# A fused attention, Fourier mixing and feed-forward kernel: slots replaced by a list scheduler, weights converted in two VectorE passes

## The chip, the cores and the metric

One core of a Trainium2 chip runs the program, in one launch. The metric is device time in microseconds: the median of the runs shown. The core's engines are TensorE (PE in the profile; its weight loads are PEld), VectorE (DVE), ScalarE (ACT), GpSimd (POOL) and SyncE (SP), which issues all DMAs. Each engine works through its own instructions in order and waits on semaphores for the others.

## The reference

```python
# batch 8, heads 8, 512 local and 32 global tokens, head size 64
s_g  = scale * q_g @ concat(k_g, k_l).T          # 32 global queries see everything
out_g = softmax(s_g) @ concat(v_g, v_l)
s_l  = concat(scale * q_l @ k_g.T, where(|i - j| <= 32, scale * q_l @ k_l.T, -1e9))
out_l = softmax(s_l) @ concat(v_g, v_l)
x = concat(out_g, out_l)                         # (8, 544, 512) after joining the heads
u = x + real(fft(fft(x, axis=1), axis=2))        # mixing over tokens and channels
un = (u - mean) / sqrt(var + 1e-6)
out = u + relu(un @ w_ch1) @ w_ch2               # 512 -> 2048 -> 512
```

All is float32 for the host; the weights reach the kernel as pairs of 32-bit words of a 64-bit float, and the kernel converts them itself. For precision nearly every factor of a matmul is a sum of two float16 parts (hi and lo), so that a product takes three matmuls (hi·hi, hi·lo, lo·hi).

## The kernel before

**The stages.** *Attention* goes by pairs of heads, 4 pairs a batch, 32 in all; a pair has 4 units of 128 queries. For a unit: `scores` (PE) into one PSUM tile S, `masked` (line 409, DVE: add the mask, take the row minimum of the negated values), `exps` (line 418, ACT), `p_hi` (422, ACT) and `p_lo` (426, POOL) split the probabilities, `turn` (431, SP) transposes them by DMA into `pl`, `values` (447, 449, PE) multiplies with V into a PSUM bank, `norm` (458 to 460, DVE) divides. S has one buffer for two units and is shared with the global queries' scores (`g_scores`, `g_exp` on lines 482 and 483). Results go to DRAM (`xs`). *The Fourier mixing* of a batch loads `xs` again (lines 582 to 588 and 550 to 559), folds it with additions on DVE and POOL (`d_odd`, `d_even`, `d_tail`), multiplies with cosine and sine tables (`d_first`, `d_second`) and adds into `u`. *The feed-forward* goes by 17 chunks of 256 tokens. A chunk needs statistics, normalised rows (`l_un`, `l_lo` on line 780) turned by DMA (`l_turn`), then 8 steps of `f_first` (line 812: 24 matmuls of 256 columns), `f_hi` (817, ACT), `f_lo` (821, DVE) and `f_second` (831: 12 matmuls of 512 columns), and ends with line 836 and the store.

**The weights** are 32 tiles of 128x512 numbers (16 for each matrix). For a tile, `w_load` (178) fetches 512 KB, `w_abs` (186, ACT) takes the high word's magnitude into PSUM, and `w_bits` makes four passes on DVE (lines 194 to 197): a maximum with an accumulator, a shift, and two that put the bits of a float32 together. `w_max`, `w_fold` and `w_scale` find a power of two for a block of 512 columns by way of a PE transpose. `w_hi` (252, ACT) then makes the hi part. The lo part of the first matrix takes two POOL passes (259, 263), that of the second one DVE pass (261). All 32 tiles of both matrices have to be through before a chunk can end.

**The order.** A table written by hand gives every call a slot and a rank in it; `Plan.run` sorts all calls by that time and records them in this order, and each engine's program is what falls to it. The first chunk has slot 37 (`F0`); each step of the feed-forward has a fixed place between attention steps:

```python
for fp in range(8):
    t = F + 2 * fp
    at(t + .30, self.f_first, c, fp)
    at(t + .97, self.f_hi, c, fp)
    at(t + 1.20, self.f_lo, c, fp)
    at(t + 3.30, self.f_second, c, fp)
```

Counted in PE's order, 1022 matmuls of attention, mixing and scales stand ahead of the first `f_first`, and 3899 behind it; the feed-forward has 3264 on line 812 and 1632 on line 831.

Of the kernel before, what the change touches and what calls it, by code (L numbers as in the profile page):

```python
# [74 lines left out]

class Plan:
    def __init__(self, warp):
        self.q, self.warp = [], warp

    def add(self, slot, rank, fn, *a):  # L80
        self.at(self.warp(slot + rank), fn, *a)

    def at(self, time, fn, *a):
        self.q.append((time, len(self.q), fn, a))

    def run(self):
        for *_, fn, a in sorted(self.q, key=lambda e: e[:2]):
            fn(*a)
# [951 lines left out]
```

## Time and profile before

| | us |
|---|---|
| three runs | 1143.2, 1146.0, 1149.0 (median 1146.0) |
| span of the profiled execution | 1140.9 |
| median less the span | 5.1 |
| first matmul of the feed-forward starts | 219.6 |
| last result of the feed-forward is written | 1132.3 |
| one chunk of 17 where nothing else runs on PE | 41.7 |

The profiled execution's own time, with what lies around its span, is not shown apart; the runs are 2.3 to 8.1 us longer than its span, and the median 5.1. The profile has a page (busy time of each engine, a row of 40 slices), the timeline of instructions, a list of waits with what ended them, groups of equal instructions with their mean, and sums over chosen stretches. In a row of a group, `out<-in` names tiles, and behind the bar stand total busy time, the mean of one in ns, and the idle time before. PE's busy time has modelled ends, so that a stretch that reads 100% busy still can be slower than its matmuls allow; the distance from start to start of a stage is the safer number.

### The profile page before, as it was taken

What the parts mean: (1) busy time and instruction counts of PE and PEld (TensorE: products, weight loads), DVE (VectorE), ACT (ScalarE), POOL (GpSimd) and SP (SyncE); (2) the same over time, 40 slices, a digit from 0 to 9 for tenths busy, and PEclk for the clock granted to TensorE, in tenths of its full rate; (3) what the DMA queues carried; (4) which work ended last, traced back from release to release, by engine and by line L of the source; (5) the groups of instructions that cost most, each with busy time, mean ns of one, the idle gap of its engine ahead of it and who ended that gap; (6) DMA issues with size and microseconds to landing.
All of it is one profiled execution on the core that took longest, in us unless ns stands there. A gap on an engine that the chain in (4) does not pass through costs nothing.

```text
span 1140.9 us, 25333 instructions
## 1 busy us (share of the span) xinstructions
PE 962.4 (84%) x9831; PEld 683.1 (60%) x9831; DVE 715.2 (63%) x1884; ACT 622.1 (55%) x1350; POOL 558.9 (49%) x712
## 2 busy tenths in 40 slices
PE   0244326597999899999999999999999999999996
PEld 0133215465666676667766676766667766666664
DVE  6997898768775847495749574947494453413211
ACT  5768558688676566666656665666564212212210
POOL 3789375758566745574557455645473212201100
PEclk9997556599999999999999999999999999999998
DMA  7478966568569483748365936583645212011100
GB/s 272 148 153 229 272 164 140 137 132 165 119 138 197 68 192 68 180 77 192 65 178 81 178 79 177 81 189 67 132 84 126 52 58 74 16 47 38 19 20 19
DMA packets 249569, 137.63 MB, mean 121 GB/s; under 512 B 200576, under 2 KB 223200, under 8 KB 249448
## 3 DMA queue, kind: packets, MB, share of 16 engines
q1 hardware_dynamic: 249448, 136.01, 52.2%
q8 instruction: 77, 1.26, 0.5%
q14 instruction: 44, 0.36, 0.1%
HBM read 65.10 MB, written 18.35 MB: 73 GB/s over the span
## 4 chain that ended last, share of the span: by engine, by line
PE 51%; DVE 26%; ACT 7%; DMA 7%; issue 4%; POOL 3%; SPq 1%; DVEq 0%; POOLq 0%; ACTq 0%
PE acc L831 21%; PE ps L812 21%; DVE pe L409 2%; ACT pe L418 2%; PE S L399 2%; DMA xt<-xs 2%; DVE h L821 2%; PE bk L708 2%; DVE ps L195 1%; DVE z L329 1%; DVE ps L194 1%; DVE ps L196 1%; PE S L469 1%; DVE z L319 1%; DVE wm L197 1%
## 5 line engine op out<-in xcount | busy, mean ns | idle before, releaser
L812 PE MATMUL ps<-uh,wh 128*128 128x256 f16 x3264 | 382.5, 274 | 0.0
L831 PE MATMUL acc<-wh,h 128*128 128x512 f16 x1632 | 377.8, 381 | 2.3 <-DVE u L836 2.2
L812 PEld LDWEIGHTS <-wh 128*128 128x128 f16 x3264 | 318.8, 98 | 58.9 <-issue 0.6
L831 PEld LDWEIGHTS <-h 128*128 128x128 f16 x1632 | 153.7, 99 | 172.5 <-issue 8.8
L426 POOL TENSOR_TENSOR ph<-pe,ph 128x448 f16<-128x448 f32 x128 | 135.7, 1060 | 162.1 <-ACT ph L422 98.5
L821 DVE SCALAR_TENSOR_TENSOR h<-ps,h 128x512 f16<-128x512 f32 x136 | 93.3, 686 | 184.4 <-ACT h L817 183.9
L817 ACT ACTIVATE h<-ps 128x512 f16<-128x512 f32 x136 | 80.1, 589 | 222.4 <-PE ps L812 222.3
L418 ACT ACTIVATE pe<-pe,nm 128x224 f32<-128x224 f32 x256 | 102.0, 469 | 75.3 <-DVE nm L409 75.2
L409 DVE CUSTOM_DVE_ANT_0 pe<-S,msk,z 128x224 f32<-128x224 f32 x256 | 99.6, 446 | 3.1 <-PE S L399 2.5
L447 PE MATMUL bk<-vN,pl 128*128 128x65 f16 x768 | 72.9, 203 | 31.5 <-DMA pl<-ph 14.6
L399 PE MATMUL S<-kT,qT 64*128 64x192 f16 x768 | 56.5, 273 | 40.1 <-ACT pg L483 35.7
L399 PEld LDWEIGHTS <-qT 64*128 64x128 f16 x1536 | 54.8, 102 | 45.5 <-issue 37.1
L447 PEld LDWEIGHTS <-pl 128*128 128x128 f16 x768 | 62.2, 104 | 22.2 <-DMA pl<-ph 16.6
L422 ACT ACTIVATE ph<-pe 128x448 f16<-128x448 f32 x128 | 72.0, 563 | 0.0
L449 PEld LDWEIGHTS <-pl 96*128 96x128 f16 x768 | 60.0, 104 | 18.5 <-issue 11.7
L765 POOL TENSOR_SCALAR ve<-ve 128x2 f32<-128x2 f32 x17 | 5.7, 338 | 113.8 <-DVE ve L764 112.8
L377 POOL TENSOR_TENSOR kT<-qk,kT 128x512 f16<-128x512 f32 x32 | 42.0, 1312 | 38.2 <-ACT kT L372 33.6
L724 DVE SCALAR_TENSOR_TENSOR asm<-bk,dsc,asm 128x258 f32<-128x258 f32 (+1 forms) x21 | 10.1, 482 | 75.1 <-PE bk L708 60.5
L449 PE MATMUL bk<-vB,pl 96*128 96x65 f16 x576 | 54.9, 203 | 0.0
L775 ACT ACTIVATE un<-u,ve 128x512 f32<-128x512 f32 x34 | 27.6, 811 | 49.0 <-DVE unh L780 39.0
L362 ACT ACTIVATE qk<-qk,z 128x512 f32<-128x512 f32 x64 | 45.2, 708 | 11.7 <-DVE z L327 11.7
L352 POOL TENSOR_TENSOR vN<-vf,vN 128x640 f16<-128x640 f32 x32 | 46.7, 1459 | 2.2 <-ACT vN L348 2.2
(188 smaller groups left out, 1626.9 us busy)
## 6 DMA issues: line engine op xcount, KB each, us to landing
qk<-in_qk SPq DMA_DIRECT2D x32, 512.0 KB
vf<-in_v SPq DMA_DIRECT2D x32, 320.0 KB
raw<-in_moe_w_ch SPq DMA_DIRECT2D x18, 512.0 KB
xs<-x SPq DMA_DIRECT2D x32, 256.0 KB
out<-u SPq DMA_DIRECT2D x16, 512.0 KB
rw<-in_moe_w_ch SPq DMA_DIRECT2D x12, 512.0 KB
x<-xs SPq DMA_DIRECT2D x24, 256.0 KB
u<-xs SPq DMA_DIRECT2D x24, 256.0 KB
```

The costliest lines, as they stand in the source:

```text
L352: self.nc.gpsimd.tensor_sub(vN[:, :, 1, :, 0:64], self.st[p]["vf"], vN[:, :, 0, :, 0:64])
L399: nc.tensor.matmul(ps, qT[r, a, j], k, start=m == 0, stop=m == 2)
L409: nc.vector.tensor_tensor_reduce(self.per[(4 * p + j) % 4][:, h, 0:224], S[:, h, 224 * n:224 * n + 224], self.msk[:, j], z[:, 8:9], 3e38, ...
L418: nc.scalar.activation(pe[:, h, 0:224], pe[:, h, 0:224], AF.Exp, bias=nm[:, n, h:h + 1], scale=-1.0)
L422: self.nc.scalar.activation(ph[:, 0, :, 0:224], self.per[i % 4][:, :, 0:224], AF.Copy)
L426: self.nc.gpsimd.tensor_sub(ph[:, 1, :, 0:224], self.per[i % 4][:, :, 0:224], ph[:, 0, :, 0:224])
L447: nc.tensor.matmul(pv[:, j % 2, h], pl[:, 4 * a + 2 * h], vN[:, j, c, h, :], start=m == 0, stop=False)
L449: nc.tensor.matmul(pv[:, j % 2, h], pl[0:96, 4 * a + 2 * h + 1], vb, start=False, stop=m == 2)
L812: nc.tensor.matmul(ps[:, q], wt[:, w, c0:c0 + P], uh[:, :, 4 * a + kt, :], start=n == 0, stop=n == 11)
L817: self.nc.scalar.activation(h[:, 0], self.fps, AF.Relu)
L821: self.nc.vector.scalar_tensor_tensor(h[:, 1], self.fps, 0.0, h[:, 0], op0=ALU.max, op1=ALU.subtract)
L831: nc.tensor.matmul(self.acc_f[j], h[:, a, q, j * P:(j + 1) * P], self.w[1, f][:, w, :], start=f == 0 and a == 0 and w == 0, stop=f == 15 a ...
```

## The change

**The scheduler.** Every call becomes a job with an engine, a duration written into the code (us), the objects that it reads and writes, and for some a target time `t`. Rings of buffers are declared with their sizes. `Plan.run` plays the jobs through: it takes the engine that can start earliest, among its jobs that are ready at that moment the one with the earliest target, and books its end; a DMA also waits its turn in one serial queue and gets 2.0 us on top. The jobs are recorded in the order of these starts. Jobs without a target get one from what reads them. The feed-forward's matmuls have 10,000 added to their target, so that they stand only where nothing else of PE is ready; jobs of PE count as ready 0.6 us later than their inputs (0.3 for the feed-forward). The two work banks of PSUM become a pool that jobs take in turn.

**The weights.** ACT writes the scaled magnitude to PSUM (`w_split64`) and the low word's upper three bits as an integer to SBUF (`w_low`, new). DVE makes two passes: `w_size` joins them (one input in PSUM, one in SBUF), `w_sign` adds the sign (both inputs in SBUF). The scale comes from a sum over the columns' magnitudes: a matmul of a constant with the upper half of each word, read as bfloat16 (`w_sum`, one per tile, 32 in all), and one reduction over 512 columns for each block of four tiles (`w_max`). `w_fold`, `w_scale` and the transpose are gone. The lo part of both matrices is made by one DVE pass (`w_lo`, both tensors in SBUF), so that POOL has none of it.

Counted in the orders of the engines: PE has 965 other matmuls ahead of the first `f_first` and 3955 behind it. On DVE, up to the pass that completes the first chunk's rows (`l_lo` for its second half; row 448 before, row 388 after in the lists below), 128 passes of `w_bits` become 32 of `w_size`, 32 of `w_sign` and 30 of `w_lo` (of the old lo passes none stands there), with 48 softmax passes in the place of 56. On ACT up to that point come 32 `w_low` and 14 more `w_hi`, and 8 fewer `exps`.

```diff
-W0 = -8
-F0 = 37
-PAUSE = 6
-LAG = 1
...
+T0 = 150.0
+STEP = 5.25
+PERIOD = 109.0
+U_AT, U_PACE = 16.0, 4.0
...
+        def ready(j):
+            t = j.hold
+            if j.prev is not None and j.prev.start is None:
+                return None
+            for d in j.deps:
+                t = max(t, d.end + self.HOP + j.margin)
+            for d in j.war:
+                t = max(t, d.end + self.HOP)
...
+                s = max(free[e], min(x[0] for x in v))
...
+            j = min((x for x in v if x[0] <= s + 1e-9), key=lambda x: (x[1].t, x[1].n))[1]
+            j.start = s
+            free[e] = s + j.us
+            if j.svc:
+                dma = max(dma, s + j.us) + j.svc
+                j.end = dma + self.LAND
+            else:
+                j.end = s + j.us
...
+    def emit(self):
+        for j in self.order:
+            j.fn(*j.a)
...
-    def w_abs(self, k, i):
+    def w_split64(self, k, i):
...
-        self.nc.scalar.activation(m.bitcast(F32), self.raw[k, i][:, :, 1].bitcast(F32), AF.Abs)
-
-    def w_bits(self, k, i):
-        nc = self.nc
-        j = i % 4 * 4 + i // 4 if k == 0 else i
-        (m, w), raw = self.w[k, i], self.raw.pop((k, i))
-        hw, lw = raw[:, :, 1], raw[:, :, 0]
-        g = m.bitcast(F32)
-        nc.vector.tensor_scalar(g, g, 2.0 ** -15, None, op0=ALU.max, op1=ALU.max, accum_out=self.mx[k][:, j:j + 1])
-        nc.vector.tensor_scalar(m, m, 3, 0x3FFFFFF8, op0=ALU.logical_shift_left, op1=ALU.bitwise_and)
-        nc.vector.scalar_tensor_tensor(m, hw, -0x40000000, m, op0=ALU.bitwise_and, op1=ALU.bitwise_or)
-        nc.vector.scalar_tensor_tensor(w, lw, 29, m, op0=ALU.logical_shift_right, op1=ALU.bitwise_or)
...
+        act.activation(m, self.raw[k, i][:, :, 1].bitcast(F32), AF.Abs, scale=2.0 ** -112)
+
+    def w_low(self, k, i, n):
+        t = self.p1.tile([P, 512], I32, name="lw", tag=("un", "xf", "xm")[n % 3])
+        self.wt[k, i] = t
+        self.nc.scalar.activation(t, self.raw[k, i][:, :, 0].bitcast(U32), AF.Copy, scale=2.0 ** -29 - 2.0 ** -47, bias=7.5 * 2.0 ** -18 - 0.5)
+
+    def w_size(self, k, i):
+        (w, m), t = self.wv.pop((k, i)), self.wt.pop((k, i))
+        self.nc.vector.scalar_tensor_tensor(w, m.bitcast(I32), 3, t, op0=ALU.logical_shift_left, op1=ALU.bitwise_or)
+        self.w[k, i] = w
+
+    def w_sum(self, k, i):
+        n = i // 4 if k == 0 else i % 4
+        c = i % 4 if k == 0 else i // 4
+        if n == 0:
+            self.wl[k, c] = self.ps.tile([P, 512], F32, name="wl", tag=f"acc{c % 2}")
+        b = self.w[k, i].bitcast(BF16).rearrange("p (n t) -> p n t", t=2)
+        self.nc.tensor.matmul(self.wl[k, c], self.partb, b[:, :, 1], start=n == 0, stop=n == 3)
+
+    def w_sign(self, k, i):
+        w, raw = self.w[k, i], self.raw.pop((k, i))
+        self.nc.vector.scalar_tensor_tensor(w, raw[:, :, 1], -0x80000000, w, op0=ALU.bitwise_and, op1=ALU.bitwise_or)
...
-    def w_fold(self):
...
+    def w_lo(self, k, i):
+        f, s, w = self.wf.pop((k, i))
+        self.nc.vector.scalar_tensor_tensor(w[:, 1], f, s, w[:, 0], op0=ALU.mult, op1=ALU.subtract)
...
-    def w_split(self, k, i):
-        nc = self.nc
-        f, s, w = self.w_hi(k, i)
-        if k == 0:
-            nc.gpsimd.tensor_mul(f, f, s.to_broadcast([P, 512]))
-        else:
-            nc.vector.scalar_tensor_tensor(w[:, 1], f, s, w[:, 0], op0=ALU.mult, op1=ALU.subtract)
-            return
-        nc.gpsimd.tensor_sub(w[:, 1], f, w[:, 0])
...
+            add("SP", .44, self.w_load, k, i, n, w=rw + ([("wload",)] if n == 31 else []), svc=1.6)
+            add("ACT", .62, self.w_split64, k, i, r=rw, w=[w, m], t=T)
+            add("ACT", .66, self.w_low, k, i, n, r=rw, w=[lw], t=T + .5)
+            add("DVE", .70, self.w_size, k, i, r=[m, lw], w=[w], t=T + 1.5)
+            wl = (f"acc{c % 2}", "w", k, c)
+            add("PE", .45, self.w_sum, k, i, r=[w], w=[wl] + end, t=T + 2)
+            add("DVE", .75, self.w_sign, k, i, r=rw + [w], w=[w], t=T + 2)
...
+            add("ACT", .71, self.w_hi, k, i, r=[w, ws], w=[h], t=T)
+            add("DVE", .89, self.w_lo, k, i, r=[w], w=[h], t=T + 1)
...
+            add("PE", PEF * .8, self.scores, i, r=[kT, qT, kg], w=[S], t=U[2 * h], margin=PEM)
+            for n in range(2):
+                u = 4 * p + 2 * h + n
+                pe, ph = ("pe", u), ("ph", u)
+                add("DVE", 1.06, self.masked, u, r=[S, z, ("msk",)], w=[pe, ("nm", u)])
+                add("ACT", .94, self.exps, u, r=[pe, ("nm", u)], w=[pe])
+                add("ACT", .565, self.p_hi, u, r=[pe], w=[ph])
+                add("POOL", 1.06, self.p_lo, u, r=[pe, ph], w=[ph])
+                add("SP", 1.26, self.turn, u, r=[ph], w=[("pl", u)], svc=1.0, margin=SPM)
...
+            t = 1e4 + T + STEP * fp
...
+            add("PE", 2.63, self.f_first, c, fp, r=[uh, ("wend",)] + w1, w=[ps], t=t, back=False, margin=.3)
+            add("ACT", .59, self.f_hi, c, fp, r=[ps], w=[h], t=-1e3, back=False)
+            add("DVE", .69, self.f_lo, c, fp, r=[ps, h], w=[h], t=-1e3, back=False)
+            add("PE", 2.6, self.f_second, c, fp, r=[h] + w2, w=acc, t=t + 1.4 * STEP, back=False, margin=.3)
```

The first place is DVE's order while the weights are converted, somewhere in the first pair's attention. Before, one tile's four passes on the PSUM tile `ps` stand together, between `norm`'s three and the softmax:

```order
135 L194 TENSOR_SCALAR ps_570,mx_92<-ps_570 128x512
136 L195 TENSOR_SCALAR ps_570<-ps_570 128x512
137 L196 SCALAR_TENSOR_TENSOR ps_570<-raw,ps_570 128x512
138 L197 SCALAR_TENSOR_TENSOR wm<-raw,ps_570 128x512
139 L458 TENSOR_SCALAR dn<-bk_127,z 128x4
140 L459 RECIPROCAL dn<-dn 128x4
141 L460 TENSOR_TENSOR x<-bk_127,dn 128x256
142 L409 ISA pe_88,nm<-S,msk,z 128x224
```

After, the same stretch holds one or two passes a tile, with lo parts (line 395) between them:

```order
117 L349 SCALAR_TENSOR_TENSOR wm<-ps_650,lw 128x512
118 L395 SCALAR_TENSOR_TENSOR wh<-wm,wsc,wh 128x512
119 L362 SCALAR_TENSOR_TENSOR wm<-rx,wm 128x512
120 L349 SCALAR_TENSOR_TENSOR wm<-ps_709,lw 128x512
121 L604 TENSOR_SCALAR dn<-bk_122,z 128x4
122 L605 RECIPROCAL dn<-dn 128x4
123 L606 TENSOR_TENSOR x<-bk_122,dn 128x256
124 L362 SCALAR_TENSOR_TENSOR wm<-raw,wm 128x512
125 L395 SCALAR_TENSOR_TENSOR wh<-wm,wsc,wh 128x512
126 L349 SCALAR_TENSOR_TENSOR wm<-ps_754,lw 128x512
```

Four passes (194 to 197) have become line 349 (`w_size`) and line 362 (`w_sign`), some instructions apart, and line 395 has come in from GpSimd.

The second place is DVE's order around the first chunk's `l_lo`, which `l_turn` and then the first `f_first` wait for. Before (line 780 is `l_lo`, 261 a lo part of the second matrix):

```order
446 L332 TENSOR_SCALAR z<-z 128x2x2
447 L333 TENSOR_SCALAR z<-z,ge 128x2
448 L780 TENSOR_TENSOR unh<-un,unh 128x512
449 L512 TENSOR_SCALAR dng<-bk_127,z 64x1
450 L513 RECIPROCAL dng<-dng 64x1
451 L514 TENSOR_SCALAR xg<-bk_127,dng 64x64
452 L261 SCALAR_TENSOR_TENSOR wh<-wm,wsc,wh 128x512
```

After (line 945 is `l_lo`, 395 a lo part, 621 to 623 the global maximum, 604 to 606 `norm`):

```order
379 L395 SCALAR_TENSOR_TENSOR wh<-wm,wsc,wh 128x512 x2
380 L945 TENSOR_TENSOR unh<-un,unh 128x512
381 L604 TENSOR_SCALAR dn<-bk_122,z 128x4
382 L605 RECIPROCAL dn<-dn 128x4
383 L606 TENSOR_TENSOR x<-bk_122,dn 128x256
384 L621 TENSOR_REDUCE ng<-S 64x1
385 L622 TENSOR_REDUCE ng<-S 64x1
386 L623 TENSOR_SCALAR ng<-ng,z 64x1
387 L395 SCALAR_TENSOR_TENSOR wh<-wm,wsc,wh 128x512 x2
388 L945 TENSOR_TENSOR unh<-un,unh 128x512
```

The second matrix's lo parts now stand ahead of the first chunk's rows, where they stood behind them.

The third place is SP's order where the second batch's mixing is loaded. Before (582 to 588 load the folded rows, 431 transposes a unit's probabilities, 786 a chunk's rows):

```order
156 L300 DMA qk<-in_qk 128x1024
157 L304 DMA vf_74<-in_v 128x640
158 L582 DMA x_3160<-xs_132 128x512
159 L584 DMA x_3160<-xs_132 128x512 x2
160 L540 DMA x_3160<-xs_132 112x512
161 L541 DMA x_3160<-xs_132 16x512
162 L586 DMA xt<-xs_132 15x512
163 L587 DMA xt<-xs_132 15x512
164 L588 DMA xt<-xs_132 2x512
165 L786 DMA_TRANSPOSE uh<-unh 128x8x128
166 L431 DMA_TRANSPOSE pl<-ph 128x8x128
```

After (732 to 742 and 686, 687 the same rows, 698 and 699 the next loads, 577 the unit's transposes):

```order
143 L639 DMA_TRANSPOSE plg<-pgr 128x10x64
144 L732 DMA x_3112<-xs_127 128x512
145 L734 DMA x_3112<-xs_127 128x512 x2
146 L686 DMA x_3112<-xs_127 112x512
147 L687 DMA x_3112<-xs_127 16x512
148 L740 DMA xt<-xs_127 15x512
149 L741 DMA xt<-xs_127 15x512
150 L742 DMA xt<-xs_127 2x512
151 L698 DMA u<-xs_127 128x512
152 L699 DMA u<-xs_127 128x512
153 L577 DMA_TRANSPOSE pl<-ph 128x8x128 x2
154 L408 DMA gn<-in_g 128x384
```

The block of eight issues is the same before and after; two loads of `u` (698, 699) have moved up directly behind it, ahead of the next transposes, and the loads for the next pair (300, 304) have moved away from in front of it.

## Rows read from the trace of the kernel before

**Rows 1.** The page: span, engines' busy time, PE's tenths in 40 slices.

```profile
span 1140.9 us, 25333 instructions
...
PE 962.4 (84%) x9831; PEld 683.1 (60%) x9831; DVE 715.2 (63%) x1884; ACT 622.1 (55%) x1350; POOL 558.9 (49%) x712
...
PE   0244326597999899999999999999999999999996
```

**Rows 2.** Busy time by stretch; the first row names the columns.

```profile
core 0: us, PE busy (x) PEld busy (x) DVE busy (x) ACT busy (x) POOL busy (x), PEclk, DMA share, GB/s
0.00:206.00 206.00, 72.91 (x982) 58.25 (x983) 173.35 (x473) 136.88 (x301) 130.93 (x135) 0.75 0.71 191
219.60:300.00 80.40, 70.20 (x827) 51.34 (x823) 62.46 (x167) 62.97 (x139) 56.27 (x69) 0.93 0.60 123
300.00:640.00 340.00, 327.93 (x3556) 232.57 (x3555) 232.02 (x629) 218.43 (x488) 197.64 (x246) 0.99 0.64 136
640.00:914.00 274.00, 269.47 (x2887) 190.97 (x2886) 168.71 (x460) 152.03 (x333) 139.09 (x185) 1.00 0.55 113
914.00:1131.50 217.50, 217.49 (x1536) 146.63 (x1533) 67.17 (x122) 41.19 (x68) 27.25 (x72) 1.00 0.13 36
1045.40:1087.10 41.70, 41.70 (x290) 28.20 (x289) 10.30 (x18) 7.55 (x12) 3.58 (x15) 1.00 0.10 26
```

**Rows 3.** The timeline: start, duration, engine, line, operation, count.

```profile
219.61 4.72 PE L812 MATMUL ps<-uh,wh 128*128 128x256 f16 x24
...
1126.15 5.34 PE L831 MATMUL acc<-wh,h 128*128 128x512 f16 x24
...
1131.53 0.75 DVE L836 SCALAR_TENSOR_TENSOR u<-acc,ve,u 128x512 f32<-128x512 f32 x1 [0.48 <-PE acc L831]
```

**Rows 4.** PE's waits (total, times, longest): to 219.6, then after it.

```profile
PE bk L447 <- DMA pl<-ph: 14.6, 6, 5.2
...
PE S L399 <- ACT pg L483: 11.4, 5, 5.9
PE bk L447 <- DVE xg L514: 6.9, 5, 1.5
```

**Rows 5.** The timeline of VectorE: the four passes over one weight tile.

```profile
142.70 0.70 DVE L194 TENSOR_SCALAR_CACHE_REDUCE ps<-ps 128x512 f32<-128x512 f32 x1
...
143.50 0.70 DVE L195 TENSOR_SCALAR ps<-ps 128x512 int32<-128x512 int32 x1
144.23 0.69 DVE L196 SCALAR_TENSOR_TENSOR ps<-raw,ps 128x512 int32<-128x512 int32 x1
144.96 0.69 DVE L197 SCALAR_TENSOR_TENSOR wm<-raw,ps 128x512 int32<-128x512 int32 x1
```

**Rows 6.** Groups of instructions: busy us, mean ns of one, idle before, releaser.

```profile
L409 DVE CUSTOM_DVE_ANT_0 pe<-S,msk,z 128x224 f32<-128x224 f32 x256 | 99.6, 446 | 3.1 <-PE S L399 2.5 <-POOL wh L263 0.6
...
L475 DVE TENSOR_REDUCE ng<-S 64x1 f32<-64x512 f32 x32 | 21.5, 673 | 7.0 <-PE S L470 7.0
...
L261 DVE SCALAR_TENSOR_TENSOR wh<-wm,wsc,wh 128x512 f16<-128x512 f32 x16 | 13.5, 845 | 4.7 <-ACT wh L252 4.7
...
L197 DVE SCALAR_TENSOR_TENSOR wm<-raw,ps 128x512 int32<-128x512 int32 x18 | 12.4, 686 | 0.6
...
L418 ACT ACTIVATE pe<-pe,nm 128x224 f32<-128x224 f32 x256 | 102.0, 469 | 75.3 <-DVE nm L409 75.2
...
L252 ACT ACTIVATE wh<-wm,wsc 128x512 f16<-128x512 f32 x32 | 22.7, 709 | 0.0
...
L186 ACT ACTIVATE ps<-raw 128x512 f32<-128x512 f32 x18 | 11.2, 621 | 15.9 <-DMA raw<-in_moe_w_ch 10.0 <-DVE wm L197 4.3 <-DVE ps L195 1.6
```

**Rows 7.** Line 644 (min/median/max ns), and the timeline where it meets GpSimd.

```profile
L644 DVE TENSOR_TENSOR st<-xt x8: 408/1670/2361, 147.9 to 928.9; 32x255 f32<-32x255 f32 x8
...
147.52 2.35 POOL L594 TENSOR_TENSOR s<-x 128x1020 f32<-128x1020 f32 x1
...
147.86 2.27 DVE L644 TENSOR_TENSOR st<-xt 32x255 f32<-32x255 f32 x1
```

More of the change, by code (lines that the diff above doesn't have):

```diff
@@ L73, in shape_constants, with __init__ @@
     return {"c1": c1, "c1t": c1t, "c2": c2, "alt": alt, "msk": m}
-class Plan:
[L77 to L84, printed above, removed]
-    def run(self):
-        for *_, fn, a in sorted(self.q, key=lambda e: e[:2]):
-            fn(*a)
+class Job:
+    def __init__(self, eng, us, fn, a):
+        self.eng, self.us, self.fn, self.a = eng, us, fn, a
+        self.deps, self.war, self.alloc = [], [], []
+        self.t, self.svc, self.margin, self.back, self.hold = None, 0.0, 0.0, True, 0.0
+        self.start = self.end = None
@@ L168, in w_load @@
     def w_load(self, k, i, n):
-        if n > 23 and n % 3 == 2:
+        if RAW[n % 7] == "u":
             raw = self.p2.tile([P, 512, 2], I32, name="rx", tag="u", bufs=3)
-        elif n < 24 and n % 4 < 2:
-            if n == 0:
+        elif RAW[n % 7] == "rw":
+            if "rw" not in self.raw:
                 rw = self.p1.tile([P, 2, 512, 2], I32, name="rw", tag="x4")
-                self.rw = [rw[:, j] for j in range(2)]
-            raw = self.rw[n % 2]
+                self.raw["rw"] = [rw[:, j] for j in range(2)]
+            self.raw["rw"].reverse()
+            raw = self.raw["rw"][1]
         else:
@@ L228, in w_scale @@
-    def w_scale(self, k, c):
-        nc = self.nc
-        nc.tensor.matmul(self.wpb, self.part[0:1], self.wmx, start=True, stop=True)
+        v = self.mx2[:, c:c + 1]
+        nc.vector.tensor_reduce(v, self.wl.pop((k, c)), axis=EX, op=ALU.max)
+        nc.vector.tensor_scalar_max(v, v, TINY)
+        if k == 1:
+            if c < 3:
+                return
+            nc.vector.tensor_mul(self.mx2[:, 0:4], self.mx2[:, 0:4], self.wsc[:, 0:4])
+            v = self.mx2[:, 4:5]
+            nc.vector.tensor_reduce(v, self.mx2[:, 0:4], axis=EX, op=ALU.max)
+            nc.vector.tensor_scalar_max(v, v, TINY)
@@ L431, in turn, with bank @@
         self.nc.sync.dma_start_transpose(pl, self.phr[i % 3].rearrange("p a h c -> p (a h c)"))
-    def bank(self, i):
-        return self.bk1 if i % 4 and not (i > 31 and i % 16 > 7) else self.bk
+    def bank(self, o):
+        return (self.bk, self.bk1)[self.plan.slot[o]]
     def values(self, i):
@@ L825, in f_second @@
         if fp == 0:
-            self.acc_f = [self.ps.tile([P, DM], F32, name=f"acc{j}") for j in range(2)]
+            self.acc_f[c] = [self.ps.tile([P, DM], F32, name=f"acc{j}") for j in range(2)]
         for j in range(2):
@@ L966, in run @@
[L966 to L987 removed]
+            c = t // 4
```

662 lines of the change are left out of this document (423 added, 239 removed).

## The prediction

> **What bounds the kernel now.** I read the page first: PE has 962.4 of 1140.9 us, and its row of tenths tells that the share is an average over two stages: low digits in the first seven slices, nines from then on [rows 1]. The stretches give the size. To 206 us PE is busy for 73 us and VectorE for 173 of 206, the most of any engine; ScalarE has 137, GpSimd 131 [rows 2]. From 219.6 us, where the first feed-forward matmul starts, to 1131.5 us, where the last one ends (the write of its result starts then) [rows 3], PE is busy in all but 10.2 + 12.1 + 4.5 + 0.0 = 26.8 us of 911.9 [rows 2]. So there are two terms: when the feed-forward can start, which VectorE sets, and how long PE needs from there, which hardly has holes.
>
> In the second term the work is fixed. A chunk with nothing beside it takes 41.7 us (the last row of [rows 2]), 17 chunks take 708.9. The 3899 other matmuls behind the start have the rest: 911.9 - 26.8 - 708.9 = 176.2 us, 0.045 each. The holes are named in the list of waits: PE waits for S until `g_exp` has read it (11.4 us, 5 times), for a work bank until `norm` or `g_norm` has read it (6.9 us), and smaller ones [rows 4]. Behind the last matmul lie 9.4 us to the end of the span.
>
> **The change part by part.** *The start.* Counted in the orders, up to the first chunk's last `l_lo`.
>
> Removed: one tile's four passes run from 142.70 to 144.96 + 0.69 = 145.65 us, 2.95 us a tile [rows 5]; 32 tiles, 94.4 us. Eight fewer softmax passes at 99.6/256 = 0.39 us [rows 6], 3.1 us.
>
> Added on VectorE: `w_size` has the operands of the old line 197 (one tensor in PSUM, one in SBUF) and I take its 0.69 us and the 0.04 us between two passes: 32 x 0.73 = 23.4. `w_sign` and `w_lo` have two SBUF tensors. No weight pass of before had, but line 261, which is `w_lo`, has 0.845 us on average and 13.5 us for 16 [rows 6]; with the gap 0.885, so 32 x 0.885 = 28.3 for `w_sign` and 30 x 0.885 = 26.6 for `w_lo`. Eight reductions over 512 columns at 0.67 us (line 475, 64 partitions, is the nearest row [rows 6]): 5.4. The small instructions of scales, statistics and norms that come and go differ by a few either way; I cost them at nothing, since the engine is busy anyway and they cancel to about a microsecond.
>
> The sum on VectorE: 94.4 + 3.1 - 23.4 - 28.3 - 26.6 - 5.4 = 13.8 us less. If the passes with two SBUF tensors ran at 0.73, it would be 23. The other side is line 644, also two SBUF tensors: 0.41 us at its shortest, 1.67 at the median, and 2.27 where it started at 147.86 beside a GpSimd instruction of 147.52 to 149.87, so that it ended with that one [rows 7]. At 1.26 us more for each of 62 passes VectorE would have 78 us more than the 23 saved, 55 us more than before. I take a value near the two rows that are most like the new passes (197 and 261), 18 us less, since GpSimd loses its two passes a tile for the first matrix and is in the way less.
>
> On this the Trainium skill has a rule: its page "GPSIMD Engine Reference", section "Specifications", says that GpSimd shares its SBUF interfaces with VectorE and contends with VectorE instructions that have two SBUF inputs. Line 644 agrees. The page gives no price; by the rule every one of the 62 passes can meet it, and by the old passes none could; the sums for both are the 55 us more and the 23 us less above.
>
> ScalarE is next: 136.9 us + 32 `w_low` at 0.62 (line 186, the same read; a PSUM output there and an SBUF output here, so 0.71 of line 252 is the other bound [rows 6]) + 14 `w_hi` at 0.71 - 8 `exps` at 102.0/256 = 0.40 = 163 us. In 188 us that is 87%, a little over VectorE's 84% now; it hides, but barely. If it doesn't hide, at 84% it needs 194 us, and the start is 6 us later. The 32 `w_sum` go to a PE that is idle for two thirds of that time. The DMAs of the weights are the same 32.
>
> So the first `f_first` starts at 219.6 - 18 = 201.6, I take 202; bounds 185 (VectorE's idle 33 us of the 206 shrinks too) and 220, no gain; the contention above is a case of its own.
>
> *From the start on.* 3955 other matmuls stand behind it, 56 more: 2.5 us. The holes: in the new order a feed-forward group stands wherever no other job of PE is due, with 0.6 us of margin, so PE has work where it now waits for S. The durations in the code are over what the rows show: two softmax passes are booked as 1.06 us against 0.78, two `exps` as 0.94 against 0.80 [rows 6], so results will tend to be there before the order wants them. Against it: the new order packs the attention denser (its last matmuls stand in chunk 11, not in chunk 13), and the booked DMA time is a guess. Nothing in the trace shows a hole of the new order, so I bound it: 0, and 26.8 as now; I take 10, nearer to the stretch from 640 to 914 us (4.5 us in 274) than to the one from 219.6 to 300 (10.2 in 80) [rows 2].
>
> The sum, against the profiled execution: 202 + 708.9 + 176.2 + 2.5 + 10 + 9.4 = 1109.0 us of span, where now it is 219.6 + 911.9 + 9.4 = 1140.9. The median of the runs is 5.1 us over that span, so 1114.1: I predict 1114 us.
>
> **The rivals.** *A, more is gained.* VectorE loses its idle time as well and the holes vanish: 185 + 708.9 + 176.2 + 2.5 + 0 + 9.4 + 5.1 = 1087 us. For it: the durations booked too long, and a PE that is idle for 27 us today only because its order was written by hand. Against: ScalarE at 163 us of 185 would have to run nearly without a gap, and its inputs come by DMA.
>
> *B, nothing is gained.* The start is held by something that didn't change: the chain from the first batch's last `norm` by DRAM to the mixing and back, and ScalarE; and the holes stay as they are. 219.6 + 911.9 + 2.5 + 9.4 + 5.1 = 1148.5. Against it: VectorE is busy for 84% of that stretch, and holes have no reason to stay the same.
>
> *C, slower: the transposes come late.* PE's order is fixed, and `values` stands where the code's DMA times say that `pl` has landed. The mixing of a batch issues ten DMAs of rows in one block now, and the next units' transposes queue behind them on SP. Today a wait for `pl` took up to 5.2 us (the first row of [rows 4]), in the start stage. If two units of each of the seven batches still to come wait so long, that is 73 us, 1114 + 73 = 1187 us. From some 5.4 us a batch on (38 us in all) the kernel is slower than now. For it: such waits do exist, 14.6 us in 6 of them, and attention and mixing are denser than before. Against: behind 219.6 us there is none of note in the list.
>
> *D, slower: contention.* With line 644's price the start goes to 219.6 + 55 = 275, and the sum to 1187 as well; from about 20 us more than before on VectorE it is slower. Its size is bounded by line 261's mean, which was taken beside a GpSimd at work in 56 of 80 us [rows 2] and is only 0.16 over line 197. This is the result of the page's rule named above if each pass waits for a whole GpSimd instruction.
>
> **How the numbers follow.** The forecast has a chance of 0.62, and by its bounds (a start 10 us either way, holes of 0 to 26) lies between 1094 and 1140; A 0.16; B 0.08; C 0.09; D 0.05. About 0.5%, 6 us, is what a measurement of this kernel can tell from no change: below 1140 is faster, above 1152 slower. A and the forecast are faster but for its upper edge, 0.77; B and that edge are the same, 0.09; C and D 0.14. The range holds 8 in 10 if it leaves out C, D and the lower part of A: 1087 to 1146.
>
> **What would show it.** The start of the first feed-forward matmul (202; 220 is B, 275 D); the mean of the passes with two SBUF tensors (0.85; over 1.2 is D) and ScalarE's busy share up to there; PE's idle time between the start and the last matmul (10; 27 is B, over 50 C) and which releaser the longest waits have (a DMA into `pl` is C); from start to last matmul 898 us. I am wrong if the start is early and the time is not, or if a stretch with no holes takes longer than its matmuls, as then the 0.045 us or the 41.7 us were not fixed.

## The result and the profile after

The changed kernel takes 1101.5 us in the median (1100.3 to 1105.7) where the kernel before took 1146.9; the ratio is 0.960, with a 95% interval of 0.957 to 0.964. That is 45 us less. The forecast was 1114, with 1087 to 1146. The time lies 13 us under the forecast, inside its range, and the experiments below show that one of the two reasons given for the gain was not the right one. (One of the four runs of e7 below took 3135.0 us; its ratio leaves that run out, its median of 1094.2 does not, and is 1093.7 without it.)

The page of the changed kernel, as in [rows 1]:

```profile
span 1098.8 us, 25376 instructions
...
PE 963.0 (88%) x9848; PEld 672.1 (61%) x9848; DVE 676.5 (62%) x1796; ACT 641.6 (58%) x1382; POOL 526.6 (48%) x679
...
PE   2545253999899899999999989999999999999996
```

PE's work is the same to 1 us (963.0 for 962.4). The nines begin in the eighth slice of a shorter span.

The stretches, with the columns of [rows 2], from the first feed-forward matmul on and ahead of it:

```profile
0.00:193.10 193.10, 80.29 (x973) 54.64 (x974) 168.26 (x416) 162.75 (x347) 111.73 (x117) 0.71 0.81 214
193.10:300.00 106.90, 103.47 (x1185) 74.70 (x1185) 74.17 (x210) 79.62 (x185) 72.01 (x78) 0.97 0.66 144
300.00:640.00 340.00, 332.46 (x3809) 234.94 (x3806) 237.61 (x696) 242.08 (x538) 214.40 (x278) 0.99 0.66 144
640.00:914.00 274.00, 271.48 (x2686) 190.26 (x2685) 158.47 (x418) 131.91 (x274) 118.50 (x175) 1.00 0.45 96
914.00:1089.30 175.30, 175.30 (x1204) 117.61 (x1202) 37.22 (x62) 25.26 (x41) 9.96 (x34) 1.00 0.10 29
```

PE's idle time behind the start is 3.4 + 7.5 + 2.5 + 0.0 = 13.5 us, where it was 26.8. Ahead of the start VectorE is busy for 168 of 193 us and ScalarE for 163, so that both are at 84 to 87%.

The summary of line 977 (`f_first`; minimum, median and maximum in ns, then the first and last start), and the end of the timeline, as in [rows 3]:

```profile
L977 PE MATMUL ps<-uh,wh x3264: 269/273/418, 193.1 to 1083.9; 128*128 128x256 f16 x192
...
1084.00 5.34 PE L996 MATMUL acc<-wh,h 128*128 128x512 f16 x24
...
1089.38 0.75 DVE L1001 SCALAR_TENSOR_TENSOR u<-acc,ve,u 128x512 f32<-128x512 f32 x1 [0.48 <-PE acc L996]
```

The feed-forward starts at 193.1, for 219.6, and needs 1089.3 - 193.1 = 896.2 us, for 911.9. So 26.5 us of the gain lie ahead of the start and 15.7 behind it.

The longest waits of PE behind the start, as in [rows 4]:

```profile
PE S L549 <- DVE nm L557: 4.4, 2, 3.1
PE bk L862 <- DVE x L606: 2.9, 1, 2.9
PE bk L593 <- DVE dsc L720: 1.8, 1, 1.8
PE ps L977 <- DMA uh<-unh: 1.4, 1, 1.4
...
PE bk L593 <- DVE xg L660: 0.9, 1, 0.9
```

The wait for S until `g_exp` had read it (11.4 us) is gone; what PE still waits for at S is `masked` (`nm`, 4.4 us). The wait for a bank until `g_norm` has read it (`xg`) is 0.9 us for 6.9, while two others, of 2.9 and 1.8 us, stand in the list. No wait for `pl` is among them.

The weight passes of VectorE up to the start, as in [rows 5, 6] (busy us, mean ns, idle before):

```profile
L395 DVE SCALAR_TENSOR_TENSOR wh<-wm,wsc,wh 128x512 f16<-128x512 f32 x32 | 30.1, 957 | 0.0
...
L349 DVE SCALAR_TENSOR_TENSOR wm<-ps,lw 128x512 int32<-128x512 int32 x32 | 21.6, 681 | 0.4 <-ACT lw L345 0.2
L362 DVE SCALAR_TENSOR_TENSOR wm<-rx,wm 128x512 int32<-128x512 int32 x13 | 11.5, 891 | 2.7 <-PE wl L358 2.7
L362 DVE SCALAR_TENSOR_TENSOR wm<-raw,wm 128x512 int32<-128x512 int32 x10 | 8.0, 798 | 0.8 <-PE wl L358 0.7
L362 DVE SCALAR_TENSOR_TENSOR wm<-rw,wm 128x512 int32<-128x512 int32 x9 | 7.0, 775 | 0.1
```

`w_size` has 0.681 us, `w_sign` (11.5 + 8.0 + 7.0)/32 = 0.83 and `w_lo` 0.957. `w_size` and `w_sign` are within 0.02 us of the forecast's 0.69 and 0.845, `w_lo` is 0.11 over it.

The path to the start is read from four places: the first `scores`, the first load of the mixing (line 582 before, 732 after), the end of the first chunk's second `l_lo`, and the first `f_first`. The first three, of before and then of after (in the rows with three durations the start is the first number behind them; a row of the timeline begins with its start):

```profile
L399 PE MATMUL S<-kT,qT x204: 239/362/365, 37.1 to 226.2; 64*128 64x192 f16 x102
L582 SPq DMA_DIRECT2D x<-xs x1: 326/326/326, 137.2 to 137.2; - x1
...
207.14 0.69 DVE L780 TENSOR_TENSOR unh<-un,unh 128x512 f16<-128x512 f32 x1
```

```profile
L549 PE MATMUL S<-kT,qT x204: 239/352/365, 21.0 to 221.1; 64*128 64x192 f16 x102
L732 SPq DMA_DIRECT2D x<-xs x1: 332/332/332, 119.2 to 119.2; - x1
...
187.30 0.68 DVE L945 TENSOR_TENSOR unh<-un,unh 128x512 f16<-128x512 f32 x1
```

From these rows: the attention begins 16.1 us earlier; from there to the mixing's load there are 98.2 us for 100.1; from the load to the last `l_lo` 68.8 for 70.6; from there to the first matmul 5.1 for 11.8. That adds to 16.1 + 1.9 + 1.8 + 6.7 = 26.5. The first term of this sum is the largest, and it is a matter of order: the slots put eight weight tiles ahead of the first scores, and the scheduler puts the scores where their inputs are ready.

VectorE's busy time up to the end of that `l_lo`, before and then after (third number of busy time, behind PE and PEld):

```profile
0.00:207.80 207.80, 72.91 (x982) 58.25 (x983) 175.02 (x481) 138.65 (x305) 130.93 (x135) 0.75 0.71 191
0.00:188.00 188.00, 78.46 (x941) 52.99 (x943) 163.45 (x397) 157.65 (x336) 107.40 (x105) 0.72 0.80 213
```

It has 11.6 us less to do, and 8.2 us less of idle time.

### The profile page after: what moved, and what is told of

Read it like the earlier page. It is cut to its first block, busy times and chain, and to the rows that moved or that the text cites. A ratio compares the mean times of both kernels' runs of the same rounds, so it can differ in the third digit from the quotient of the medians.

```text
span 1098.8 us, 25376 instructions
## 1 busy us (share of the span) xinstructions
PE 963.0 (88%) x9848; PEld 672.1 (61%) x9848; DVE 676.5 (62%) x1796; ACT 641.6 (58%) x1382; POOL 526.6 (48%) x679
## 5 line engine op out<-in xcount | busy, mean ns | idle before, releaser
L572 POOL TENSOR_TENSOR ph<-pe,ph 128x448 f16<-128x448 f32 x128 | 139.7, 1102 | 124.3 <-ACT ph L568 82.0
L564 ACT ACTIVATE pe<-pe,nm 128x224 f32<-128x224 f32 x256 | 105.4, 468 | 23.9 <-DVE nm L557 23.9
L593 PE MATMUL bk<-vN,pl 128*128 128x65 f16 x768 | 70.7, 201 | 16.1 <-DVE xg L660 9.4
L549 PEld LDWEIGHTS <-qT 64*128 64x128 f16 x1536 | 52.2, 100 | 44.7 <-issue 26.6
L568 ACT ACTIVATE ph<-pe 128x448 f16<-128x448 f32 x128 | 69.3, 564 | 4.3 <-DMA pl<-ph 3.7
L635 POOL TENSOR_TENSOR pgr<-pg,pgr 64x576 f16<-64x576 f32 x32 | 42.4, 1324 | 50.5 <-ACT pgr L632 49.8
L358 PE MATMUL wl<-wm,partb 128*128 128x512 bf16 x32 | 18.3, 578 | 41.0 <-DVE wm L349 40.9
L491 POOL TENSOR_TENSOR vf<-vf,z 128x640 f32<-128x640 f32 x32 | 42.9, 1354 | 2.0 <-DVE z L466 1.9
L886 POOL TENSOR_TENSOR u<-u,asm 128x257 f32<-128x257 f32 x16 | 11.9, 741 | 66.4 <-DMA u<-xs 48.3
L527 POOL TENSOR_TENSOR kT<-qk,kT 128x512 f16<-128x512 f32 x32 | 39.4, 1233 | 6.9 <-ACT kT L522 5.4
```

The lines of the kernel that those rows point to most:

```text
L549: nc.tensor.matmul(ps, qT[r, a, j], k, start=m == 0, stop=m == 2)
L564: self.nc.scalar.activation(pe[:, h, 0:224], pe[:, h, 0:224], AF.Exp, bias=nm[:, h:h + 1], scale=-1.0)
L568: self.nc.scalar.activation(ph[:, 0, :, 0:224], self.per[i % 4][:, :, 0:224], AF.Copy)
L572: self.nc.gpsimd.tensor_sub(ph[:, 1, :, 0:224], self.per[i % 4][:, :, 0:224], ph[:, 0, :, 0:224])
L593: nc.tensor.matmul(pv[:, j % 2, h], pl[:, 4 * a + 2 * h], vN[:, j, c, h, :], start=m == 0, stop=False)
```

## The experiments

Theory 1 was the forecast's: VectorE's amount of work sets the start. The rivals: ScalarE, the DMAs, the recorded order, or the chain of attention and mixing (the first batch's scores, softmax, transposes and results, then its mixing, each of which needs the one before). All runs, with the places named above (us; the stretch is from the first `f_first` to the last matmul's end; times are medians, and each ratio below is against runs of the kernel before taken together with it, whose medians lie between 1147.4 and 1149.2):

| kernel | first scores | mixing's load | last l_lo | first f_first | stretch | time |
|---|---|---|---|---|---|---|
| before | 37.1 | 137.2 | 207.8 | 219.6 | 911.9 | 1146.9 |
| after | 21.0 | 119.2 | 188.0 | 193.1 | 896.2 | 1101.5 |
| e1 after, no sign pass | 20.6 | 116.9 | 184.6 | 190.8 | 897.5 | 1099.5 |
| e2 after, no low pass | 20.4 | 118.2 | 187.5 | 192.7 | 899.4 | 1103.3 |
| e3 slots, new weights | 35.8 | 136.0 | 205.8 | 217.6 | 920.3 | 1148.2 |
| e4 scheduler, old weights | 25.8 | 150.0 | 220.7 | 224.5 | 905.0 | 1137.3 |
| e5 after, neither pass | 20.1 | 111.8 | 179.5 | 185.2 | 899.3 | 1094.4 |
| e6 after, half the loads | 20.8 | 118.5 | 187.2 | 192.4 | 897.0 | 1100.7 |
| e7 after, sums out of PSUM | 20.7 | 119.6 | 182.0 | 189.2 | 892.3 | 1094.2 |
| e8 before, first group early | 37.3 | 137.8 | 208.2 | 215.4 | 921.9 | 1146.7 |
| e9 after, another order | 25.5 | 113.5 | 185.8 | 190.3 | 889.1 | 1090.0 |
| e10 e9 and e7 | 25.3 | 113.6 | 179.9 | 185.9 | 889.0 | 1082.8 |
| e11 e10, attention spread | 26.7 | 119.3 | 178.4 | 185.9 | 893.1 | 1091.0 |
| e12 e4, no sign pass | 25.9 | 138.5 | 207.4 | 211.2 | 902.8 | 1122.4 |

The places are those of each one's profiled execution, which can lie some us from its median: where both times of one execution are shown, the run is 1.8 to 2.5 us longer than its span, so that the profile of before is of a run of some 1143 us, about 4 under its median.

**e1, e2, e5: VectorE and ScalarE relieved under the new order.** The order stays as it was planned with these passes. The edits, alone in e1 and e2 and both in e5:

```diff
-        self.nc.vector.scalar_tensor_tensor(w, raw[:, :, 1], -0x80000000, w, op0=ALU.bitwise_and, op1=ALU.bitwise_or)
```

```diff
-        self.nc.scalar.activation(t, self.raw[k, i][:, :, 0].bitcast(U32), AF.Copy, ...)
+        self.wt[k, i] = self.raw[k, i][:, :, 1]
```

> The changed kernel without the 32 sign passes (w_sign, 26.5 us of VectorE in its trace); the weights lose their signs, and every other instruction keeps its place. Theory 1, VectorE sets the start of the feed-forward: it comes 15 to 26 us earlier than 193.1, at 167 to 178, and the span is shorter by as much. Rival 1, ScalarE (163 of 193 us busy) or the weights' DMAs set it: at most 5 us earlier, 188 to 193. Rival 2, the chain of the first batch's mixing sets it, whatever the engines have to do: nothing, 193.

> The changed kernel without the 32 ScalarE passes w_low (20.8 us); w_size takes the high word in their place, so that the weights' values are others; every other instruction keeps its place. Theory 1, VectorE sets the start and ScalarE hides: at most 6 us earlier than 193.1. Rival 1, ScalarE sets it: 12 to 20 us earlier, 173 to 181. If both this and the run without the sign passes gain several us, the two engines hold it in turn.

> The changed kernel without the sign passes and without w_low together (26.5 us of VectorE and 20.8 us of ScalarE; the weights' values are others), all other instructions in their places. Theory 2, the two engines hold the first batch's attention in turn, each being busy for 88 to 95% of it: now the first batch's loads for the mixing are issued 10 us earlier than at 119, and the start comes at 175 to 183. Rival 5, the DMAs hold it (their share is 1.00 to 80 us): the loads at 114 to 119, the start at 187 to 193. Rival 2, only the chain of attention and mixing counts: the same as rival 5, with less than 1.0 of DMA.

Measured: 2.3, 0.4 and 7.9 us earlier at the start. Theory 1 falls for the changed kernel in its order: 23.6 us less of VectorE up to the start (144.6 us busy for 168.3) buy 2.3. Of ScalarE alone nothing comes either. Together they move the mixing's load by 7.4 us, which each alone moves by 2.3 and 1.0; the start, at 185.2, lies between the two ranges that were expected of e5. Busy time of VectorE and ScalarE in e1 and then in e5, each up to its start (columns of [rows 2]):

```profile
0.00:190.80 190.80, 80.99 (x973) 54.41 (x974) 144.64 (x385) 163.08 (x349) 108.51 (x118) 0.66 0.81 217
```

```profile
0.00:185.20 185.20, 81.89 (x974) 54.67 (x975) 143.45 (x385) 146.69 (x316) 107.04 (x117) 0.65 0.82 223
```

In e5 both are at 77 to 79%, and still 47 us of passes gave 8. So the two do hold the first part in turn, as the theory formed after e1 and e2 has it, but for 8 us and no more. That leaves the order and the chain for the rest; the DMAs are next.

**e6: the DMAs.** Half of each tile is fetched and read twice by a broadcast:

```diff
-        self.nc.sync.dma_start(raw.rearrange("p n t -> p (n t)"), self.w_src(k, i).bitcast(I32))
+        self.nc.sync.dma_start(raw[:, 0:256].rearrange("p n t -> p (n t)"), self.w_src(k, i).bitcast(I32)[:, 0:512])
```

> The changed kernel with half of each weight tile fetched (256 KB for 512) and read twice, so that the engines do the same work on other weights; all instructions in their places. Rival 5, the DMAs set the pace up to 115 us: the transposes land earlier, the loads for the mixing are issued 8 to 15 us earlier than at 119 and the start is at 178 to 186. Theory 2, engines: within 4 us of 119 and of 193.

Measured: the load at 118.5 and the start at 192.4, so that rival 5 falls. The same stretch of the changed kernel and of e6 (DMA share and GB/s are the last two numbers):

```profile
20.00:105.00 85.00, 43.04 (x503) 26.49 (x501) 76.96 (x201) 78.07 (x160) 43.24 (x33) 0.81 1.04 261
```

```profile
20.00:105.00 85.00, 43.10 (x503) 27.23 (x501) 78.56 (x201) 78.34 (x160) 42.92 (x33) 0.74 0.78 183
```

A share of 1.04 looked like a bound. With 0.78 every engine does the same within 2 us in this stretch, and no place in the table moves by more than 0.8 us.

**e3, e4: one half of the change alone.** In e3 the table of slots calls the new weight functions (`w_low` behind `w_split64`, `w_size`, `w_sum` and `w_sign` in the place of `w_bits`, `w_max` one slot later, `w_hi` and `w_lo` in that of `w_split`). In e4 the scheduler has the old ones as jobs:

```diff
-            add("DVE", .70, self.w_size, ...)
-            add("DVE", .75, self.w_sign, ...)
+            add("DVE", 2.95, self.w_bits, k, i, r=rw + [m, w], w=[w, ("mx", k, c if k == 0 else 0)], t=T + 1.5)
...
-            add("DVE", .89, self.w_lo, k, i, r=[w], w=[h], t=T + 1)
+            add(*((("POOL", 2.15) if k == 0 else ("DVE", .89)) + (self.w_lo, k, i)), r=[w], w=[h], t=T + 1)
```

> The kernel before with its slots, and the new weights alone: two VectorE passes, column sums on PE, both lo parts on VectorE. Theory 1: the start comes about 18 us earlier than 219.6, at 200 to 206, the holes behind it stay at 27 us, and the time is 1146 - 18 = 1128 (1122 to 1134). Rival 3, the scheduler gives the gain: the start stays at 215 to 220 and the time at 1141 to 1147.

> The scheduler with the weights as before: four VectorE passes, the scale by way of a transpose, the first matrix's lo part on GpSimd. Theory 1: VectorE has about 18 us more to do ahead of the start, so 206 to 214 and a time of 1114 to 1123. Rival 3, the scheduler alone gives the gain: 193 to 197 and 1101 to 1106. Rival 4, the slots were as good: 217 to 222 and over 1125.

Measured: e3 has a ratio of 1.000 (0.998 to 1.002), e4 of 0.992 (0.989 to 0.994). The halves alone give 0 and 10 us, and together 45. Both expectations of theory 1 missed, and so did that of rival 3 for e4: the slots turn no freed VectorE time into an earlier start, and the scheduler with the old weights starts 5 us later than the slots did. What the scheduler gives by itself lies behind the start: PE is idle there for 905.0 - 887.8 = 17.2 us in e4, where it is 26.8 in the kernel before and 32.0 in e3. The stretch from 40 to 160 us, of e3, e4 and the changed kernel:

```profile
40.00:160.00 120.00, 45.86 (x587) 33.12 (x587) 91.37 (x231) 91.45 (x201) 63.29 (x52) 0.74 0.76 191
```

```profile
40.00:160.00 120.00, 38.08 (x518) 30.20 (x518) 114.81 (x296) 75.86 (x162) 77.66 (x73) 1.00 0.66 185
```

```profile
40.00:160.00 120.00, 55.37 (x686) 37.75 (x687) 110.12 (x274) 102.64 (x221) 62.54 (x48) 0.66 0.82 206
```

In e3 no engine is busy for more than 91.5 of 120 us: its first scores stand at 35.8, and the places in the table stay where they were. In e4 VectorE has 114.8 of 120, and the first batch's attention, begun at 25.8, needs 124 us to the mixing's load, where it needs 98 after the change.

**e12: the sign pass left out under the old weights**, which is e1's edit in e4:

```diff
-        nc.vector.scalar_tensor_tensor(m, hw, -0x40000000, m, op0=ALU.bitwise_and, op1=ALU.bitwise_or)
```

> The scheduler with the weights as before (start 224.5, 1137.3 us), without the pass that puts the sign in: 32 passes of 0.70 us and their gaps, 23 us of VectorE; the weights lose their signs and everything else keeps its place. It is the edit of the first run, on the old weights. Theory 1 in its narrowed form, VectorE sets the start while it has the four passes (115 of 120 us busy from 40 to 160 us): the start is 14 to 23 us earlier, at 201 to 211, and the time at 1114 to 1124. Rival 2, the recorded order and the chain set it here too: at most 5 us earlier, and 1132 to 1138.

Measured: the start is 13.3 us earlier, just short of the narrowed theory's 14 to 23, and the time 14.9 us less, inside its band; both are far from its rival. From 40 to 160 us VectorE is now busy for 104.8 us, where it had 114.8 in e4:

```profile
40.00:160.00 120.00, 42.35 (x592) 32.99 (x584) 104.78 (x286) 81.37 (x172) 87.84 (x79) 1.00 0.74 204
```

The same 32 passes that are worth 2 us under the new weights are worth 13 to 15 under the old ones. So with four passes VectorE sets the start under the scheduler, and with two, in the order planned for them, it doesn't any more.

**e7: contention on the path.** In the changed kernel the mixing's last additions (lines 893 and 894) have two SBUF inputs on VectorE and stand beside GpSimd. From the two timelines, VectorE's and GpSimd's (start, duration):

```profile
165.13 4.01 DVE L893 TENSOR_TENSOR u<-u,asm 128x257 f32<-128x257 f32 x1
169.06 0.41 DVE L894 TENSOR_TENSOR u<-u,asm 128x255 f32<-128x255 f32 x1
169.40 0.42 DVE L893 TENSOR_TENSOR u<-u,asm 128x257 f32<-128x257 f32 x1
...
171.70 3.18 DVE L893 TENSOR_TENSOR xf<-xf,asm 18x257 f32<-18x257 f32 x1
```

```profile
163.98 0.72 POOL L886 TENSOR_TENSOR u<-u,asm 128x257 f32<-128x257 f32 x1
...
165.35 1.16 POOL L527 TENSOR_TENSOR kT<-qk,kT 128x512 f16<-128x512 f32 x1
...
167.83 1.03 POOL L572 TENSOR_TENSOR ph<-pe,ph 128x448 f16<-128x448 f32 x1
```

The rows left out of GpSimd's follow each other in the same way: it has no gap from 163.98 to 168.86, and VectorE's addition, begun at 165.13, ends 0.28 us behind that, while the same addition takes 0.42 beside an idle GpSimd. In e7 GpSimd adds the cosine part to the rows, and VectorE the sine part from PSUM (four passes a tile for each, where VectorE had four and GpSimd two; the durations booked for them are others, so that the order is planned anew):

```diff
-        nc.vector.tensor_add(xf[:r, 0:257], xf[:r, 0:257], Df[:, 0:257])
-        nc.vector.tensor_add(xf[:r, 511:256:-1], xf[:r, 511:256:-1], S[:, 1:256])
+            nc.vector.scalar_tensor_tensor(v, lo[:q], s0[:q], v, op0=ALU.mult, op1=ALU.add)
...
+            nc.vector.scalar_tensor_tensor(v, up[:q], s1[:q], v, op0=ALU.mult, op1=ALU.add)
```

> The changed kernel with the mixing's last additions done in another way: GpSimd adds the cosine part to the rows, VectorE adds the sine part out of PSUM (one PSUM and one SBUF input in place of two SBUF inputs). Theory 3, VectorE stands still there beside GpSimd (4.01 and 3.18 us for additions that take 0.42 alone) on the path to the first chunk: the stretch from the last matmul of the mixing to the first chunk's last l_lo falls from 21.9 us to 12 to 16, the start is at 184 to 188, and the time at 1092 to 1097. Rival: GpSimd's four additions a tile take the place, and the start stays within 2 us of 193.

Measured: 1094.2 us, ratio 0.953 (0.949 to 0.957). The groups of VectorE's additions up to the start, in e7:

```profile
L887 DVE SCALAR_TENSOR_TENSOR u<-bk,dsc,u 128x256 f32<-128x256 f32 x4 | 1.9, 478 | 0.0
L889 DVE SCALAR_TENSOR_TENSOR u<-bk,dsc,u 128x256 f32<-128x256 f32 x4 | 1.9, 474 | 0.0
```

None is longer than 0.48 us. From the mixing's last matmul to the last `l_lo` there are 11.4 us for 21.9, a little under the expected 12 to 16. But that matmul itself ends 4.6 us later (170.65 for 166.09), because the contention came back elsewhere: GpSimd, with twice the additions, has no gap from 157.95 to 165.63, and these passes on VectorE, which make the scales of an attention pair, stand beside it:

```profile
161.05 0.96 DVE L481 TENSOR_SCALAR z<-z 128x4 f32<-128x4 f32 x1
162.04 1.23 DVE L482 TENSOR_SCALAR z<-z 128x4 f32<-128x4 f32 x1
163.18 1.30 DVE L483 TENSOR_SCALAR z<-z,ge 128x2 f32<-128x2 f32 x1
164.39 0.45 DVE L852 SCALAR_TENSOR_TENSOR z<-bk,z 128x274 f16<-128x274 f32 x1
```

In the changed kernel the first three take 0.17, 0.17 and 0.22 us there, beside an idle GpSimd; in e7 line 852, for which PE waits 4.0 us, stands behind them. So the last `l_lo` ends 6.0 us earlier, and the first matmul starts only 3.9 us earlier, a little short of the expected 184 to 188: the turn of the rows stands on SP behind four DMAs of other pairs and is issued 3.0 us after the rows are there.

**e8: the tail of the slots.**

```diff
-                at(t + .30, self.f_first, c, fp)
+                at(t + .30 - (1.2 if c + fp == 0 else 0), self.f_first, c, fp)
```

> The kernel before with one edit: the first chunk's first matmul group stands directly behind the global scores, ahead of values and the next scores. Theory 4, the 11.8 us from the first chunk's last rows to its first matmul are its place in PE's order (it stands behind scores that wait for S), not the DMA: the start is at 213 to 216, and the time 2 to 5 us under 1146. Rival, the transposed rows land late: 218 to 220 and no change.

Measured: the start is at 215.4, as theory 4 has it, so that 4.6 of the 11.8 us were the place in PE's order (7.2 are left). The time did not follow: ratio 0.999 (0.997 to 1.000). The scores behind it came later, and PE's wait for S until `g_exp` had read it, 11.4 us before [rows 4], is

```profile
PE S L399 <- ACT pg L483: 15.0, 5, 5.9
```

in e8. A start moved alone is given back at the next wait.

**e9, e10, e11: the order alone.** In e9 only numbers of the planner are others (the margins, the landing time, the booked durations, of which two are shown, and the targets, which are not):

```diff
-PEM, SPM = 0.6, 0.2
+PEM, SPM = 0.2, 0.5
...
-    LAND = 2.0
+    LAND = 1.0
...
-                add("DVE", 1.06, self.masked, ...)
-                add("ACT", .94, self.exps, ...)
+                add("DVE", 0.78, self.masked, ...)
+                add("ACT", 0.84, self.exps, ...)
```

> The changed kernel with the same work and another order alone: durations booked as the trace measured them (two softmax passes 0.78 us for 1.06, two exps 0.84 for 0.94, the mixing's contended passes 4.2, 3.2 and 5.4 us for 2.4, 2.6 and 4.0), a landing time of 1.0 us for 2.0, a margin of 0.2 us for 0.6, and other targets. Theory 5, the start is set by the recorded order, not by any engine's amount of work: 182 to 188 where it is 193.1 now, the first batch's loads for the mixing at 112 to 117 where they are at 119, and 1088 to 1096 us. Rival, the chain of attention and mixing is as short as it can be: 191 to 195 and 1099 to 1104; or tighter booking makes PE wait more behind the start: over 20 us of holes and over 1104.

> That order together with the additions of the mixing out of PSUM. Theory 3 and 5 together: a start at 176 to 183, holes of 5 to 15 us, and 1080 to 1088 us; if the two gains are one and the same wait, 1091 to 1095 as with the additions alone.

> As the run before, with the later batches' attention spread over more of the feed-forward (a batch every 148 us for 105, a step every 6.0 for 5.5). If VectorE, ScalarE and DMA loads beside the feed-forward cost PE time behind the start, fewer holes and 2 to 6 us under the run before; if PE is full there anyway, within 3 us of it; if attention runs out behind the last chunks, slower.

Measured: e9 1090.0 us (ratio 0.950, 0.948 to 0.952), with the same work as the changed kernel. The start came at 190.3 and not at 182 to 188: the mixing's load is 5.7 us earlier, and the mixing then takes 72.3 us for 68.8. The larger part, 7.1 us, is in the stretch behind. e10 has 1082.8 us (0.944, 0.941 to 0.946), 19 us under the changed kernel, and is the best of all; the two gains add (11.5 and 7.3), though its start, 185.9, is behind the expected 176 to 183. e11, with the attention spread out (and a smaller margin and a longer landing time), has the same start and 1091.0 us: it costs 8 in the median, of which the profiled stretch shows 4, and the guess of 2 to 6 us less was wrong. The two stretches of e10:

```profile
0.00:185.90 185.90, 81.11 (x973) 53.60 (x974) 157.34 (x399) 156.10 (x333) 106.69 (x120) 0.65 0.76 211
185.90:1074.90 889.00, 882.10 (x8880) 616.57 (x8877) 494.26 (x1397) 487.76 (x1050) 433.03 (x608) 0.99 0.51 110
```

6.9 us of holes are left behind the start, and the 186 us ahead of it have PE busy for 81.

## Why the forecast held, and where its reasons did not

**From the start on: the mechanism was right, the number in part by two misses that cancel.** The forecast had 897.6 us, and 896.2 was measured. Its holes were 10 us and are 13.5; its matmuls were 887.6 us, and PE is busy for 882.7. The steps of `f_first` of the last chunks still start 5.21 us apart, 41.7 us a chunk, so that it is the 3955 other matmuls that take less: 173.8 us, 0.044 each. The wait for S until `g_exp` is gone as described, and that it is the scheduler that makes the holes fewer, with either weights, is shown by e3 (32.0 us) and e4 (17.2).

**The start: the step that failed is "which VectorE sets".** The sum on VectorE, 13.8 us taken as 18, gave the start, and the last `l_lo` does end 19.8 us earlier. That is luck as far as the number goes: only 11.6 of the 19.8 are less work of VectorE, the others are idle time that it lost. And it is no proof: e3 has still less work on VectorE up to there (148 us busy for 175) and moves `l_lo` by 2.0 us, e4 moves it the other way by 12.9, and e1 takes off another 24 us of VectorE for 2.3 at the start. The row of e3 up to its `l_lo`:

```profile
0.00:205.80 205.80, 77.02 (x999) 55.43 (x1000) 148.08 (x393) 155.45 (x337) 102.00 (x104) 0.79 0.72 193
```

What the runs show in its place: the scheduler begins the first batch's attention earlier (20 to 27 us for 36 to 37), and can only keep that up if VectorE is not full; with the old weights it is (e4, e12), with the new ones it isn't. The forecast put the earlier start down to the weights alone and the holes to the scheduler alone. For the holes that holds; for the start neither half pays by itself.

**The stretch behind the last rows was not in the sum.** The 11.8 us from the last `l_lo` to the first matmul were carried over unchanged; they became 5.1. With that and 2 us at `l_lo` the start is 193.1 and not 202, which is 9 of the 10 us by which the span was missed (1098.8 for 1109.0). The rest of the 13 us is the base: 5.1 us between the median and the profiled span were mostly an execution faster than the median, and the median of after lies 2.7 us over its profiled span.

**The rivals.** A (1087) was nearer in its mechanism than its price: less idle time ahead of the start and fewer holes. B: the holes did not stay. That the chain it names holds the start of the changed kernel follows from what is left when VectorE, ScalarE and the DMAs are relieved (e1, e2, e5, e6) and is not shown by itself; it runs 16 us earlier. C: no wait for `pl` is among the longest behind the start. D: the new passes stayed at 0.83 and 0.957 us, under the 1.2 that would have spoken for it. The contention that the Trainium skill's page "GPSIMD Engine Reference" (section "Specifications") names was met at another place, the mixing's additions (4.01 us for 0.42); with these out of PSUM, and an order planned anew, the kernel is 7 us faster (e7).

**Left open:** how much of e9's gain is the margins, the durations, the landing time or the targets; they were changed together. What the chain of the first batch's attention, 98 us from its first scores, would take with no weights beside it was not tried, nor whether the scheduler would start earlier if it planned without the sign pass: e1 keeps the order. And of the 31.4 us between the starts of e4 and of the changed kernel e12's pass gives 13.3; the new weights also take the first matrix's lo part off GpSimd and drop the transposes of the scales, and the shares of these were not separated.

## What to carry to other kernels

An engine that is busy for 85% is a bound only if taking work off it moves the end: take one pass away with the order kept, and see. Work taken off an engine pays where something hands the freed time on; a table of places does not (e3), and an order planned from durations does. Where two halves of a change each lift what holds the other, their gains can't be added from one trace.

## What the hardware showed that was not expected

- A VectorE instruction with two SBUF inputs made no end while GpSimd went from one instruction straight into the next: 4.01 us for 0.42, through five of them. That is one case and not a rule: in e7 a pass of `w_lo` that began at 169.40 us ended after 1.17, inside such a stretch. With one input in PSUM the mixing's additions took 0.46 to 0.48 beside GpSimd in e7. The passes of `w_size`, one PSUM and one SBUF input, were 0.681 on average; `w_lo`, with two in SBUF, 0.957.
- Passes on VectorE with one SBUF tensor of 128x4 were held up beside GpSimd as well: 0.96 and 1.23 us for 0.17 (lines 481 and 482 in e7).
- A DMA share of 1.04 over 85 us was no bound: with a quarter less of it (0.78) no place in the table moved by more than 0.8 us (e6).
